# Gate products on GpSimd and a transposed first segment: one change to a fused attention and gated-MLP kernel

## The chip, the cores and the metric

The kernel runs on one core of a Trainium2 chip. The metric is the device time of one execution in microseconds (us); the time of a kernel is the median of several executions. One execution is also recorded by the hardware profiler, and all engine times below come from that record. Engine names in the profile: PE is TensorE (matmul), PEld its weight loads, DVE is VectorE, ACT is ScalarE, POOL is GpSimd, SP is SyncE; a q behind a name is that engine's instruction queue, where DMAs are issued.

## The reference, cut to what matters

One input x (2048 x 512) goes through two branches. Branch A is attention with 32 heads of width 16 in 4 segments of 512 rows, causal inside a segment, plus a running memory (M, z) of the earlier segments. Branch B is a gated MLP. A gate per row mixes them.

```python
g = sigmoid((x * gate_w).sum(-1, keepdims=True))        # one number per row
a = A(x)                                                # attention, below
b = (gelu(x @ w_gate) * (x @ w_up)) @ w_down
out = g * a + (1 - g) * b

def A(x):
    q, k, v = x @ wq, x @ wk, x @ wv                    # split in 32 heads, 4 segments
    gb = sigmoid(beta)                                  # one number per head
    for s in range(4):
        p = softmax(q_s k_s^T / 4 + causal mask)
        a_dot = p @ v_s
        num, den = phi(q_s) @ M, phi(q_s) @ z + 1e-06   # phi(t) = t + 1 if t > 0 else exp(t)
        out_s = gb * num / den + (1 - gb) * a_dot
        M += phi(k_s)^T @ v_s;  z += phi(k_s).sum()
    return concat(out_s) @ wo
```

## The kernel before

The kernel keeps x transposed in SBUF (xT), the weights, and the hidden layer of the MLP (G). Its phases: loads and the first keys; the queries and values of segment 0; the gate-weight matmuls with gelu for all segments (until about 79 us); then attention for the four segments, with the up and down matmuls of the MLP as filler between the attention steps; last the output of segment 3.

Every step is a task with an estimated cost, an engine, predecessors and a priority. A list scheduler runs through the tasks in modelled time and so decides, when the kernel is built, in which order each engine's instructions stand. Each engine then works strictly in that order.

```python
LAT = {"PE": 220, "ACT": 130, "DVE": 130, "POOL": 150, "SP": 0, "EXT": 0}
...
def ext(at):                      # a load, with the time at which the scheduler takes it as landed
    return add("EXT", 0, lambda e: None, lat=at)
```

The loads at the start, and the turning of x for segment 0 (the other segments are turned by transposing DMAs):

```python
for h, eng in enumerate((nc.sync, nc.scalar)):
    eng.dma_start(xn[:, 2 * h:2 * h + 2, :], x0r[:, 2 * h:2 * h + 2, :])
for h, eng in enumerate((nc.sync, nc.scalar)):
    eng.dma_start(wk[:, 2 * h:2 * h + 2, :], wkr[:, 2 * h:2 * h + 2, :])
load_w(nc.sync, wq, A_wq)
nc.sync.dma_start(wga[:, :, 0:4 * P], wgr[:, :, 0:4 * P])
load_w(nc.sync, wv, A_wv)
nc.sync.dma_start(wga[:, :, 4 * P:DFF], wgr[:, :, 4 * P:DFF])
for s in range(1, NSEG):
    load_x(s)                     # 4 transposing DMAs each
nc.sync.dma_start(gw[:, :], gate_w.rearrange("(fc p) -> p fc", p=P))
nc.sync.dma_start(beta8[:, :], A_beta.rearrange("(c h) -> h c", h=8))
...
def first_k():
    ...
    # 7 matmuls on zeros ("warm"), then for each of 4 column blocks fc:
    for kt in range(KT):
        nc.tensor.matmul(tl["x", fc][:, kt * P:(kt + 1) * P],
                         lhsT=xn[:, kt, fc * P:(fc + 1) * P], rhs=ident,
                         start=True, stop=True)
    # copied to xT by VectorE and ScalarE in turn; then the key matmuls
```

One head group of attention: ScalarE's exponential of the logits (L617), a causal mask on GpSimd (`affine_select`, L626), the product with the values on TensorE ("pv"; a column of ones in v gives the softmax sum), then on VectorE:

```python
nc.vector.transpose(TT[key][:, e, :, :]..., t[:, :])            # L664: from PSUM
nc.vector.reciprocal(RR[key], TT[key][:, :, :, DH:DH + 1])      # L674: 1 / softmax sum
nc.vector.tensor_mul(RR[key][:, :, :, 0], RR[key][:, :, :, 0],  # L677: the gate factor
                     G2[:, s, :][:, None, :].to_broadcast((P, 2, QB)))
nc.vector.tensor_mul(NN[key], TT[key][:, :, :, 0:DH],           # L682: normalise
                     RR[key].to_broadcast((P, 2, QB, DH)))
nc.vector.tensor_add(NN[key], NN[key], NMt[key])                # L687: add the memory part
nc.vector.transpose(xT[:, c, s * L:(s + 1) * L], NN[key]...)    # L690
```

G2 holds the gate's factor per row. Once per segment the memory's reciprocal gets the same factor (L815), used by the products L838:

```python
nc.vector.reciprocal(RMt[s], RMt[s])                            # L812
nc.vector.tensor_mul(RMt[s], RMt[s],                            # L815
                     G2[:, s, :][:, :, None].to_broadcast((P, QB, 8)))
```

Phi is made by ScalarE and VectorE, and a sum of 1024 numbers per partition on GpSimd (L720).

Of the kernel before, what the change touches and what calls it, by code (L numbers as in the profile page):

```python
# [10 lines left out]
BF = dt.bfloat16  # L11
F32 = dt.float32

P = 128
# [5 lines left out]
L = 512  # L20
# [135 lines left out]
def kernel(  # L156
# [15 lines left out]
    nc = tc.nc  # L172
# [13 lines left out]
    plg = ctx.enter_context(tc.tile_pool(name="plg", bufs=3, space=bass.MemoryType.PSUM))  # L186
# [7 lines left out]
    add = S.add  # L194
# [4 lines left out]
    def lgtile(name="lg"):  # L199
        return plg.tile([P, 2, L], F32, name=name, tag="lg")  # L200

    def gen(name):
        return pgen.tile([P, L], F32, name=name, tag="gen")
# [11 lines left out]
    wv = ctile("wv", [P, FC, D])  # L215
# [29 lines left out]
    def load_w(eng, t, src):  # L245
        eng.dma_start(t[:, :, :], src.rearrange("(fc p) n -> p fc n", p=P))
# [13 lines left out]
    for h, eng in enumerate((nc.sync, nc.scalar)):  # L260
        eng.dma_start(wk[:, 2 * h:2 * h + 2, :], wkr[:, 2 * h:2 * h + 2, :])
    load_w(nc.sync, wq, A_wq)
    nc.sync.dma_start(wga[:, :, 0:4 * P], wgr[:, :, 0:4 * P])
    load_w(nc.sync, wv, A_wv)
    nc.sync.dma_start(wga[:, :, 4 * P:DFF], wgr[:, :, 4 * P:DFF])
    for s in range(1, NSEG):
        load_x(s)
# [5 lines left out]
    def ext(at):  # L273
        return add("EXT", 0, lambda e: None, lat=at)
# [1 line left out]
    a_xn = ext(3600)  # L276
    a_x = [None, ext(18000), ext(22000), ext(26000)]
    a_wk, a_wq = ext(3800), ext(5500)
    a_wg0, a_wv, a_wga, a_gw, a_be, a_wup, a_wo = [ext(t) for t in (8500, 10000, 14000, 27000,
                                                                    27500, 32000, 39000)]  # L280

    nc.gpsimd.memset(ident, 1.0)
    nc.gpsimd.affine_select(out=ident, in_=ident, pattern=[[-1, P]],
# [92 lines left out]
    def first_k():  # L376

        tl = {}

        def f_warm(_):  # L380
            t = lgtile("warm")
            for i in range(NWARM):
                nc.tensor.matmul(t[:, 0, :], lhsT=warm[:, 0:P], rhs=warm,
                                 start=True, stop=True)
        w = add("PE", 427 * NWARM, f_warm, prio=0, alloc=["lg"])
        add("EXT", 0, lambda _: None, deps=[w], frees=[("lg", w)])

        def f_open(_):
            a = lgtile("xt")
            for i in range(2):  # L390
                tl["x", i] = a[:, i, :]
                tl["x", 2 + i] = gen("xt")[:, :]
            for i in range(2):
                tl["k", i] = lgtile("k0")
                QK[("k", 0, i)] = rtile("kT", [P, 2, L])
        op = add("PE", 1, f_open, prio=0, deps=[w], alloc=["lg", "gen", "gen", "lg", "lg",
                                                          "kT", "kT"])
        xe = []
        prev = op
        for fc in range(FC):  # L400
            def f_t(_, fc=fc):
                for kt in range(KT):
                    nc.tensor.matmul(tl["x", fc][:, kt * P:(kt + 1) * P],
                                     lhsT=xn[:, kt, fc * P:(fc + 1) * P], rhs=ident,
                                     start=True, stop=True)
            prev = add("PE", 430, f_t, prio=1, deps=[prev, a_xn])
            xe.append(add("ACT" if fc % 2 else "DVE", 600,
                          lambda e, fc=fc: copy(e, xT[:, fc, 0:L], tl["x", fc]), prio=0,
                          deps=[prev], frees=[(("lg", 0), op) if fc < 2
                                              else (("gen", fc - 2), op)]))  # L410
        a_x[0] = xe[-1]
        TAB["wdn"] = add("SP", 600, lambda _: load_w(nc.sync, wdn, B_w_down), deps=[prev],
                         lat=40000)
        last = None
        for fc in range(FC):
            def fn(_, fc=fc):
                for c in range(NCH):
                    nc.tensor.matmul(tl["k", c // 2][:, c % 2, :],
                                     lhsT=wk[:, fc, c * P:(c + 1) * P], rhs=xT[:, fc, 0:L],
                                     start=(fc == 0), stop=(fc == FC - 1))  # L420
            last = add("PE", 4 * MM, fn, prio=2, deps=[last, xe[fc], a_wk])
            read_x[0].append(last)
        for c in range(NCH):
            first_ev[("k", 0, c // 2)] = op
            EVQK[("k", 0, c)] = add(["DVE", "ACT"], [EV["DVE"], EV["ACT"]],
                                    lambda e, c=c: copy(e, QK[("k", 0, c // 2)][:, c % 2, :],
                                                        tl["k", c // 2][:, c % 2, :]),
                                    prio=0, deps=[last], frees=[(("lg", 1 + c // 2), op)])
            odd_copy(0, c, EVQK[("k", 0, c)])
# [17 lines left out]
    TAB = {}  # L447
# [186 lines left out]
    def pv_group(s, c, e):  # L634
        g0 = s * NSLOT + 5 * c
        w0 = 0 if e == 0 else 3
        t0 = 5 * c

        def mms(t):

            for w, kt, qb, nq, at in ((w0, 0, 0, 4, 0), (w0 + 1, 1, 1, 2, 0),
                                      (w0 + 1, 1, 3, 1, 3), (2, 2, 2, 2, 2 * e),
                                      (w0 + 1, 3, 3, 1, 2)):
                for j in range(4):
                    h = 8 * c + 2 * j + e
                    nc.tensor.matmul(t[32 * j:32 * j + 32, qb * P:(qb + nq) * P],  # L646
                                     lhsT=vz[s % 2][:, kt, h * VW:h * VW + 32],
                                     rhs=pT[(s, t0 + w, j // 2)][:, j % 2, at * P:(at + nq) * P],
                                     start=(kt == 0), stop=(kt == KT - 1),
                                     tile_position=(0, 32 * j), skip_group_check=True)  # L650
        slots = [w0, w0 + 1, 2]
        deps = [AT[(g0 + w, h)] for w in slots for h in range(2)]
        deps += [EVV[(s, kt)] for kt in range(KT)] + [opened]
        if e == 1:
            deps.append(PVT[s][-1])
        def mk():
            TT[(s, c)] = rtile("T", [P, 2, QB, 32], F32)
        g, box = group("pv", 600, mms, 0.5, deps, mode="col", also=("T", mk) if e == 0 else None,
                       frees=[("pT", XT_[(g0 + w, h)]) for w in slots for h in range(2)])
        PVT[s].append(g)  # L660
        key = (s, c)

        def f_T(_, t):
            nc.vector.transpose(TT[key][:, e, :, :].rearrange("p a b -> p (a b)"), t[:, :])  # L664
        ev = evac("DVE", g, box, f_T)
        if e == 0:
            NMT[("T", key)] = g
            NMT[("Te", key)] = ev
            return
        T0 = NMT[("T", key)]  # L670

        def f_r(_):
            RR[key] = rtile("r", [P, 2, QB, 1], F32)
            nc.vector.reciprocal(RR[key][:, :, :, :], TT[key][:, :, :, DH:DH + 1])  # L674

        def f_rg(_):
            nc.vector.tensor_mul(RR[key][:, :, :, 0], RR[key][:, :, :, 0],  # L677
                                 G2[:, s, :][:, None, :].to_broadcast((P, 2, QB)))

        def f_n(_):  # L680
            NN[key] = rtile("N", [P, QB, 2, DH])
            nc.vector.tensor_mul(NN[key][:, :, :, :].rearrange("p a e d -> p e a d"),  # L682
                                 TT[key][:, :, :, 0:DH],
                                 RR[key][:, :, :, :].to_broadcast((P, 2, QB, DH)))

        def f_m(_):
            nc.vector.tensor_add(NN[key][:, :, :, :], NN[key][:, :, :, :], NMt[key][:, :, :, :])  # L687

        def f_o(_):
            nc.vector.transpose(xT[:, c, s * L:(s + 1) * L],  # L690
                                NN[key][:, :, :, :].rearrange("p a e d -> p (a e d)"))
        r = add("DVE", 280, f_r, prio=3, deps=[ev, NMT[("Te", key)]], alloc=["r"])
        rg = add("DVE", 120, f_rg, prio=3, deps=[r, TAB["g2"]])
        n = add("DVE", 650, f_n, prio=3, deps=[rg], alloc=["N"], frees=[("r", r), ("T", T0)])
        last = n
        if s > 0:
            last = add("DVE", 500, f_m, prio=3, deps=[n, NMT[("Nm", key)]],
                       frees=[("Nm", NMT[("Nm", key)])])
        OTT[key] = add("DVE", 640, f_o, prio=3, deps=[last] + read_x[s], frees=[("N", n)])
# [90 lines left out]
    def mem_den(s, prio):  # L790
# [21 lines left out]
            nc.vector.reciprocal(RMt[s][:, :, :], RMt[s][:, :, :])  # L812

        def f_g(_):
            nc.vector.tensor_mul(RMt[s][:, :, :], RMt[s][:, :, :],  # L815
                                 G2[:, s, :][:, :, None].to_broadcast((P, QB, 8)))
        ev = evac("DVE", g, box, f_T)
        a = add("DVE", 200, f_a, prio=2, deps=[ev], alloc=["rm"], frees=[("Tm", g)])
        r = add("DVE", 880, f_r, prio=2, deps=[a])
        TAB[("rm", s)] = add("DVE", 250, f_g, prio=2, deps=[r])  # L820
        TAB[("rma", s)] = a

    def mem_num(s, c, prio):
# [176 lines left out]
```

The softmax here doesn't subtract the row's maximum and nothing guards it: scores larger than these inputs give would overflow.

## Time and profile before

| | us |
|---|---|
| median of 3 runs | 290.62 (290.55 to 290.92) |
| span of the profiled execution | 289.2 |
| PE busy | 272.9 |
| DVE busy | 178.9 |
| ACT busy | 208.5 |
| POOL busy | 130.4 |

Busy is the time in which an engine had at least one instruction under way. Groups of instructions are named by line, engine and operation, then out<-in by the program's own tile names, with the count and the mean duration. A wait is named by the engine that waited and what ended it. Idle time of an engine costs something only where the engine is on the path that sets the end. The lines that carry the reading stand in the prediction.

### The profile page before, as it was taken

How to read it: one execution, taken by the hardware profiler on the slowest of the kernel's cores; microseconds unless marked ns; L12 is line 12 of the kernel's file. 1: busy time of each engine (PE TensorE's matmuls, PEld its weight loads, DVE VectorE, ACT ScalarE, POOL GpSimd, SP SyncE). 2: the span in 40 equal slices, each digit the busy share in tenths (PEclk: the TensorE clock that was granted, in tenths of full speed). 3: DMA queues.
4: the chain of work that ended last, by engine and by line, in shares of the span. 5: the costliest groups of instructions: out<-in, count | busy, mean ns of one | idle time of the engine just before them, and what ended most of it. 6: DMA issues, size and time to landing. Idle time of an engine off the chain costs nothing.

```text
span 289.2 us, 5673 instructions
## 1 busy us (share of the span) xinstructions
PE 272.9 (94%) x2279; PEld 118.4 (41%) x2320; DVE 178.9 (62%) x320; ACT 208.5 (72%) x227; POOL 130.4 (45%) x220
## 2 busy tenths in 40 slices
PE   8999999999998997999989999998899999999994
PEld 4444444444433443343334444333344344344441
DVE  2331112232197899888997786789986973869400
ACT  3634554424497998699998998999899999896021
POOL 8000000015037786755497657554855855556000
PEclk9999999999999999999999999999999999999999
DMA  7974960000001110100001330000000000000011
GB/s 239 329 124 80 368 205 2 0 0 2 0 2 36 35 25 18 39 0 2 0 2 30 27 57 20 13 8 2 0 20 20 0 20 18 22 22 18 20 36 37
DMA packets 22019, 13.74 MB, mean 48 GB/s; under 512 B 14056, under 2 KB 20968, under 8 KB 21992
## 3 DMA queue, kind: packets, MB, share of 16 engines
q1 hardware_dynamic: 21448, 12.85, 16.9%
q10 hardware_dynamic: 544, 0.52, 0.5%
q8 instruction: 18, 0.29, 0.4%
q14 instruction: 9, 0.07, 0.1%
HBM read 8.13 MB, written 2.10 MB: 35 GB/s over the span
## 4 chain that ended last, share of the span: by engine, by line
PE 68%; DVE 19%; SPq 7%; DMA 2%; issue 2%; ACT 0%; ACTq 0%
PE dn L850 17%; PE up L336 14%; PE gt L336 12%; SPq L241 7%; PE lg L594 7%; PE pv L646 6%; PE dn L855 5%; PE k L336 2%; DVE T L664 2%; PE q L336 2%; DVE G L510 2%; DVE Nm L838 2%; DVE N L682 1%; DVE Tm L834 1%; DMA wdn<-in_A_x_dram 1%
## 5 line engine op out<-in xcount | busy, mean ns | idle before, releaser
L617 ACT ACTIVATE pT<-lg 128x1024 bf16<-128x1024 f32 x160 | 154.2, 1026 | 15.2 <-PE lg L594 14.2
L626 POOL TENSOR_SCALAR_AFFINE_SELECT pT<-pT 128x512 bf16<-128x512 bf16 (+1 forms) x160 | 93.5, 595 | 71.9 <-ACT pT L617 70.9
L510 DVE TENSOR_TENSOR G<-up,G 128x512 bf16<-128x512 f32 x56 | 38.0, 683 | 41.2 <-PE up L336 41.2
L336 PE MATMUL up<-xT,wup 128*128 128x512 bf16 x213 | 55.2, 380 | 3.1 <-DVE G L510 1.9
L500 ACT ACTIVATE G<-gt 128x1024 bf16<-128x1024 f32 x28 | 28.7, 1024 | 35.9 <-PE gt L336 35.9
L850 PE MATMUL dn<-wdn,G 128*128 128x512 bf16 x213 | 52.2, 380 | 1.9 <-DVE vz_84 L183 0.8
L336 PE MATMUL gt<-xT,wga 128*128 128x512 bf16 x217 | 50.9, 379 | 0.4
L336 PEld LDWEIGHTS <-wga 128*128 128x128 bf16 x224 | 21.8, 98 | 26.3
L336 PEld LDWEIGHTS <-wup 128*128 128x128 bf16 x224 | 19.9, 97 | 27.9 <-issue 8.2
L850 PEld LDWEIGHTS <-G 128*128 128x128 bf16 x224 | 20.2, 98 | 27.0 <-issue 5.9
L471 POOL COPY G_90<-tt 32x16 f32<-32x16 f32 x16 | 3.2, 197 | 56.9 <-DVE tt L463 56.3
L664 DVE STREAM_TRANSPOSE T<-pv 128x512 f32<-128x512 f32 x32 | 22.8, 712 | 9.0 <-PE pv L646 8.9
L594 PE MATMUL lg<-qT,kT 16*128 16x256 bf16 (+2 forms) x320 | 18.7, 273 | 0.1
L594 PE MATMUL lg<-qT,kO 32*128 32x128 bf16 (+2 forms) x320 | 18.0, 272 | 0.1
L434 PE MATMUL v<-wv,xT 128*128 128x512 bf16 x61 | 15.5, 379 | 2.7 <-DVE vz_85 L183 1.6
L855 PE MATMUL dn<-wo,xT 128*128 128x512 bf16 x63 | 16.2, 379 | 0.2 <-issue 0.2
L894 ACT ACTIVATE osb<-dn,omz 128x512 bf16<-128x512 f32 x6 | 4.1, 686 | 16.6 <-PE dn L855 16.6
L336 PE MATMUL q<-xT,wq 128*128 128x512 bf16 x59 | 15.4, 380 | 0.2
L594 PEld LDWEIGHTS <-kT 16*128 16x128 bf16 x320 | 7.3, 92 | 20.0 <-issue 19.3
L682 DVE TENSOR_TENSOR N<-T,r 128x512 bf16<-128x512 f32 x16 | 14.4, 899 | 0.3
L896 DVE TENSOR_SCALAR osb<-dn,omz 128x512 bf16<-128x512 f32 x10 | 7.5, 746 | 8.8 <-PE dn L855 6.7
L594 PEld LDWEIGHTS <-kO 32*128 32x128 bf16 x320 | 7.0, 92 | 14.0 <-issue 13.7
(117 smaller groups left out, 272.3 us busy)
## 6 DMA issues: line engine op xcount, KB each, us to landing
out_dram<-osb SPq DMA_DIRECT2D x16, 128.0 KB, 1.7
wup<-in_B_w_up_dram SPq DMA_DIRECT2D x1, 1792.0 KB, 8.0
wdn<-in_B_w_down_dram SPq DMA_DIRECT2D x1, 1792.0 KB, 13.6
wga<-in_B_w_gate_dram SPq DMA_DIRECT2D x1, 1280.0 KB, 11.0
wq<-in_A_wq_dram SPq DMA_DIRECT2D x1, 512.0 KB, 6.4
wga<-in_B_w_gate_dram SPq DMA_DIRECT2D x1, 512.0 KB
wv<-in_A_wv_dram SPq DMA_DIRECT2D x1, 512.0 KB, 8.3
wo<-in_A_wo_dram SPq DMA_DIRECT2D x1, 512.0 KB, 9.1
```

Source lines behind the costliest of these rows:

```text
L241: nc.sync.dma_start_transpose(xT[:, fc, s * L:(s + 1) * L], x2[s * L:(s + 1) * L, fc * P:(fc + 1) * P])
L336: nc.tensor.matmul(t, lhsT=W[:, fc, c0:c0 + P], rhs=xT[:, fc, s * L:(s + 1) * L], start=(fc == 0), stop=(fc == FC - 1))
L500: ge = evac("ACT", g, box, lambda e, t: nc.scalar.activation(dst, t[:, :, :], AF.Gelu_apprx_tanh), cost=960, ring="lg")
L510: UPT[(s, hs)] = evac("DVE", g, box, lambda e, t: nc.vector.tensor_mul(G[:, s, hs, :], t[:, :], G[:, s, hs, :]))
L594: nc.tensor.matmul(A[j // 2][:, j % 2, at * P:(at + nq) * P], lhsT=l, rhs=r, start=True, stop=True, tile_position=(32 * j, 0))
L617: nc.scalar.activation(pT[(s, t, h)][:, :, :], A[h][:, :, :], AF.Exp, scale=0.25)
L626: nc.gpsimd.affine_select(out=v, in_=v, pattern=pat, compare_op=ALU.is_ge, fill=0.0, base=0, channel_multiplier=-1)
L646: nc.tensor.matmul(t[32 * j:32 * j + 32, qb * P:(qb + nq) * P], lhsT=vz[s % 2][:, kt, h * VW:h * VW + 32], rhs=pT[(s, t0 + w, j // 2)][:, ...
L664: nc.vector.transpose(TT[key][:, e, :, :].rearrange("p a b -> p (a b)"), t[:, :])
L682: nc.vector.tensor_mul(NN[key][:, :, :, :].rearrange("p a e d -> p e a d"), TT[key][:, :, :, 0:DH], RR[key][:, :, :, :].to_broadcast((P, 2 ...
L850: nc.tensor.matmul(t[:, :], lhsT=G[:, s, hs, qt * P:(qt + 1) * P], rhs=wdn[:, hs, :], start=(hs == 0), stop=stop and (hs == HS - 1))
L855: nc.tensor.matmul(t, lhsT=xT[:, c, s * L + qt * P:s * L + (qt + 1) * P], rhs=wo[:, c, :], start=first and c == 0, stop=(c == NCH - 1))
```

## The change

Four things differ.

1. The product with the gate factor moves from VectorE to GpSimd, for the softmax reciprocal (16 instructions) and for the memory's reciprocal (3 instructions). Its aim is to relieve VectorE. Priority and costs given to the scheduler change with it.
2. x of segment 0 is turned by TensorE's transpose operation with bf16 results in PSUM, where plain matmuls with an identity gave fp32 results.
3. The first piece of the gate weights and wv are loaded from ScalarE's queue instead of SyncE's.
4. The landing times that the scheduler assumes for these two loads change (wv 10000 to 9000, the gate piece 8500 to 10500 ns).

```diff
     load_w(nc.sync, wq, A_wq)
-    nc.sync.dma_start(wga[:, :, 0:4 * P], wgr[:, :, 0:4 * P])
-    load_w(nc.sync, wv, A_wv)
+    nc.scalar.dma_start(wga[:, :, 0:4 * P], wgr[:, :, 0:4 * P])
+    load_w(nc.scalar, wv, A_wv)
...
-    a_wg0, a_wv, a_wga, a_gw, a_be, a_wup, a_wo = [ext(t) for t in (8500, 10000, 14000, 27000,
-                                                                    27500, 32000, 39000)]
+    a_wv, a_gw = ext(9000), ext(27000)
+    a_wg0, a_wga, a_be, a_wup, a_wo = [ext(t) for t in
+                                       (10500, 14000, 27500, 32000, 39000)]
...
-            a = lgtile("xt")
+            a = plg.tile([P, 2, 2 * L], BF, name="xt", tag="lg")
             for i in range(2):
-                tl["x", i] = a[:, i, :]
-                tl["x", 2 + i] = gen("xt")[:, :]
+                tl["x", i] = a[:, i, 0:L]
+                tl["x", 2 + i] = pgen.tile([P, 2 * L], BF, name="xt", tag="gen")[:, 0:L]
...
-                    nc.tensor.matmul(tl["x", fc][:, kt * P:(kt + 1) * P],
-                                     lhsT=xn[:, kt, fc * P:(fc + 1) * P], rhs=ident,
-                                     start=True, stop=True)
+                    nc.tensor.transpose(tl["x", fc][:, kt * P:(kt + 1) * P],
+                                        xn[:, kt, fc * P:(fc + 1) * P], ident)
...
         def f_rg(_):
-            nc.vector.tensor_mul(RR[key][:, :, :, 0], RR[key][:, :, :, 0],
+            nc.gpsimd.tensor_mul(RR[key][:, :, :, 0], RR[key][:, :, :, 0],
                                  G2[:, s, :][:, None, :].to_broadcast((P, 2, QB)))
...
-        rg = add("DVE", 120, f_rg, prio=3, deps=[r, TAB["g2"]])
+        rg = add("POOL", 250, f_rg, prio=-1, deps=[r, TAB["g2"]])
...
         def f_g(_):
-            nc.vector.tensor_mul(RMt[s][:, :, :], RMt[s][:, :, :],
+            nc.gpsimd.tensor_mul(RMt[s][:, :, :], RMt[s][:, :, :],
                                  G2[:, s, :][:, :, None].to_broadcast((P, QB, 8)))
...
-        TAB[("rm", s)] = add("DVE", 250, f_g, prio=2, deps=[r])
+        TAB[("rm", s)] = add("POOL", 400, f_g, prio=-1, deps=[r])
```

## The prediction

> **What bounds the kernel now.** I read the busy shares first.
>
> ```profile
> PE 272.9 (94%) x2279; PEld 118.4 (41%) x2320; DVE 178.9 (62%) x320; ACT 208.5 (72%) x227; POOL 130.4 (45%) x220
> ```
>
> TensorE is busy for 272.9 of 289.2 us, so no other engine sets the whole span. What can be won is TensorE's idle time, 16.3 us, and it is not spread evenly. The first 1.3 us and the last 4.1 us (final copy and store) are fixed. For the rest I cut the attention part, from 79 us on, at the places where VectorE changes between running without a pause and having pauses. Columns: stretch, its length, then busy time and instruction count of PE, PEld, DVE, ACT, POOL.
>
> ```profile
> 109.00:120.30 11.30, 9.13 (x62) 3.87 (x62) 11.29 (x19) 8.71 (x10) 7.25 (x9) 1.00 0.17 35
> ...
> 134.00:155.00 21.00, 19.03 (x182) 7.73 (x186) 20.89 (x38) 19.31 (x22) 12.99 (x19) 1.00 0.00 1
> 155.00:190.00 35.00, 34.58 (x360) 15.00 (x362) 25.49 (x46) 32.55 (x36) 23.57 (x35) 1.00 0.19 32
> 190.00:209.00 19.00, 16.93 (x174) 6.94 (x177) 18.66 (x34) 17.47 (x22) 11.96 (x16) 1.00 0.00 1
> ```
>
> In three stretches VectorE never stops (11.29 of 11.3, 20.89 of 21, 18.66 of 19), and TensorE idles 2.17, 1.97 and 2.07 us there, 6.2 us together. In the stretch between, VectorE has 9.5 us to spare and TensorE idles only 0.42 us in 35. So the bound is TensorE, with three places where VectorE holds it up. The view of TensorE's waits agrees: nearly every entry names VectorE.
>
> ```profile
> PE up L336 <- DVE G L510: 1.9, 5, 1.0
> PE v L434 <- DVE vz_85 L183: 1.6, 2, 1.1
> ...
> PE dn L850 <- DVE vz_84 L183: 0.8, 1, 0.8
> PE v L434 <- DVE T L664: 0.7, 1, 0.7
> ...
> PE bps L520 <- DMA beta_78<-in_A_beta_dram: 0.6, 1, 0.6
> ```
>
> The last of these is at 29.5 us: the small beta load comes behind twelve transposing loads of x on the same queue.
>
> **The operation that moves.** The gate product on the softmax reciprocal (L677) handles 32 numbers per partition. The views of its line and of the normalising product behind it give duration min/median/max:
>
> ```profile
> L677 DVE TENSOR_TENSOR r<-r,G_90 x16: 178/344/854, 99.9 to 271.2; 128x32 f32<-128x32 f32 x16
> ```
> ```profile
> L682 DVE TENSOR_TENSOR N<-T,r x16: 679/940/1152, 100.3 to 271.4; 128x512 bf16<-128x512 f32 x16
> ```
>
> One and the same instruction takes 178 or 854 ns. The timeline says why: at 111.10 us it starts just after a causal mask has started on GpSimd, and ends just after it.
>
> ```profile
> 111.10 0.65 DVE L677 TENSOR_TENSOR r<-r,G_90 128x32 f32<-128x32 f32 x1
> ```
> ```profile
> 111.07 0.64 POOL L626 TENSOR_SCALAR_AFFINE_SELECT pT<-pT 128x512 bf16<-128x512 bf16 x1 [0.28 <-ACT pT L617]
> ```
>
> At 99.88 us, with GpSimd idle, it took 0.18 us. The Trainium skill, "SBUF — State Buffer", section "SBUF: two separate sides", states this: VectorE with two SBUF inputs and GpSimd share an exclusive port pair, and the later one waits for the whole instruction of the other. The trace agrees, 178 ns free against some 600 ns beside a mask. L682 has two SBUF inputs as well, 679 free against up to 1152.
>
> **The change part by part.**
>
> *Gate products to GpSimd.* VectorE loses 16 x 405 ns (mean of L677) = 6.5 us and 3 x 262 ns (L815) = 0.8 us, 7.3 us in all. Most of that lies where VectorE has pauses, and is worth nothing. In the three full stretches lie five of the sixteen, which took 0.65, 0.50, 0.60, 0.61 and 0.62 us by the timeline, and two of L815 at 0.25: 3.5 us. That is the ceiling of this part, as TensorE's 6.2 us there is larger.
>
> GpSimd gains 19 instructions. Its product of 1024 numbers (L720) takes 2120 ns, about 2.07 ns a number; with some 0.15 us fixed (its 32x4 copies take 182 ns) I estimate 0.2 us for 32 numbers and 0.4 us for 128, so 16 x 0.2 + 3 x 0.4 = 4.4 us on an engine at 45%. It does not become the bound. What counts is the round trip: reciprocal on VectorE, product on GpSimd, normalising product on VectorE. GpSimd may first have to finish a mask (449 or 693 ns by form) or a 2.1 us sum. I estimate 0.3 to 1 us, against 0.18 to 0.85 before. In the built order of the changed program 14 of the 16 heads have other VectorE work, mostly an up product of about 0.68 us, between reciprocal and L682, which hides it or most of it; in two there is none. Also, the mask that follows the product on GpSimd starts just when L682 is released, so port collisions can move from L677 to L682. I let these two give back over half of the 3.5 us and keep 1.5 us.
>
> The new durations also make the list scheduler issue a different order on TensorE from about 100 us on (by the times of before). On TensorE the work is the same, and so is about the number of changes between groups, 261 runs against 259; 85 down and output matmuls instead of 70 follow the last value product, so the last head's chain is covered no worse. I count the new order as 0, with an uncertainty of 2 us.
>
> *The transposes of segment 0.* Before, 7 warming matmuls and 16 plain identity matmuls come ahead of the first key matmul:
>
> ```profile
> 1.26 3.17 PE L383 MATMUL warm<-wdn 128*128 128x512 bf16 x7 [1.26 <-DVE wdn L256]
> ...
> 4.22 1.91 PE L403 MATMUL xt<-wdn 128*128 128x128 bf16 x16
> ...
> 5.32 1.29 DVE L183 CAST xT<-xt 128x512 bf16<-128x512 f32 x2 [2.90 <-PE xt L403]
> ```
>
> The seven are 0.42 us apart ((4.22 - 1.26) / 7). The same form is 0.216 us apart from about 6.8 us on: the clock has doubled. The skill, "TensorE: Matmul & The Clock Gate", "Part 4: PE-mode transpose", says that transposes don't count as busy for this clock, and its Part 1 that the clock is decided in windows of about 3.4 us. The trace of before shows the doubling some 5.3 us after the first matmul, but has no transposes to test the rest. If it holds, the clock doubles one window later, and 3.4 us of work at half speed costs 1.7 us, at the very place where TensorE is the bound. I give this 0.4: +0.7 us. The transposes themselves cost the same, 16 weight loads and 16 passes of 128 columns.
>
> Their result is now bf16 in PSUM. "VectorE: DVE Perf Modes", "Why PSUM operands drop a tier", allows two elements a cycle for 16-bit PSUM sources, one for fp32. By that the 686 ns copy becomes about 0.42 us (256 instead of 512 cycles at 0.96 GHz; an estimate from that page, no run here shows it). The first key matmul waits for the first copy, so it starts 0.27 us sooner, of which half counts at the half clock: -0.15 us.
>
> *Loads.* The first gate-weight piece and wv go out on the queue of ScalarE. That takes two issues of about 0.5 us from its free start, before its first work at 6.04 us. "DMA: Bandwidth & Descriptors", "Queues, rings and completion order", says that a DMA engine goes round-robin between queues. So wq (landing 1.82 + 6.4 = 8.2 us before) shares bandwidth with the gate piece, and may come up to 1.5 us later, near its first use at 9.83 us: +0.1 us. The SyncE queue has 1 MB less ahead of the x transposes and beta; the 0.56 us wait at 29.5 us should mostly go, also because a late TensorE would not meet it: -0.4 us.
>
> Sum: 290.6 - 1.5 + 0.7 - 0.15 + 0.1 - 0.4 = 289.35, rounded to 289.4 us.
>
> **The rivals.**
>
> *VectorE's relief comes through whole.* For it: TensorE's waits name VectorE, and 6.2 us of idle lie in full stretches. Against: the port collisions stay with L682. Time: -3.5 instead of -1.5, about 287.3 us; with a lucky order 286.
>
> *GpSimd becomes a wait of its own.* The product stands in GpSimd's queue at a place fixed in advance. If VectorE is late with the reciprocal, the masks behind it wait, then the value products on TensorE. VectorE does run later than the scheduler's costs say (an evacuation 712 ns against 610). Against: GpSimd idles 71 us waiting for ScalarE's exponentials, so it catches up. If it happened at every second head with 0.4 us: +3 us in place of -1.5, about 294 us less what buffers hide, so 292.
>
> *The slow clock alone counts.* The whole 1.7 us instead of 0.7, no gain in attention: 292 us.
>
> *Nothing reaches TensorE.* The waits only change names: 290 to 291 us.
>
> **Range and chances.** The terms are all below 2 us, and 2% is 5.8 us. The ceiling of the gain, 3.5 + 0.4 + 0.15 = 4.1 us, stays below it unless the new order helps too; a loss of 5.8 us needs the slow clock, GpSimd stalls and a bad order together. Hence 286.2 to 292.4 us for 8 in 10, faster by over 2% 0.06, slower by over 2% 0.03, the rest within.
>
> **What would show it.** Right: VectorE's busy time lower by 5 to 7 us and GpSimd's higher by 4 to 5; L677 on GpSimd near 0.2 us; TensorE's idle time in the full stretches down by 1 to 2 us; the bps wait smaller; the first copy near 0.42 us. Wrong: L682 clearly longer than its 899 ns mean, GpSimd waiting for the reciprocal, TensorE waiting in front of pv; key and query matmuls 0.43 us apart after 7 us (clock); a wait for wq. The prediction as a whole fails if the new order opens or closes TensorE waits that have nothing to do with the gate product.

## The result, and the profile after

| | before | changed |
|---|---|---|
| median, us | 290.60 | 294.27 |
| ratio to before (95% interval) | | 1.0126 (1.0113 to 1.0139) |
| span of the profiled execution, us | 289.2 | 292.3 |

The change costs 3.7 us. The time lies outside the predicted range (286.2 to 292.4), and on the other side of before than forecast.

The head of the page, which answers to the first line of the prediction:

```profile
PE 273.8 (94%) x2279; PEld 118.7 (41%) x2320; DVE 172.2 (59%) x299; ACT 209.4 (72%) x229; POOL 134.3 (46%) x239
```

VectorE has lost 6.7 us (178.9 to 172.2) and GpSimd gained 3.9 (130.4 to 134.3), as meant. The span grew all the same. The moved products and the normalising product behind them (duration min/median/max in ns, and who waited):

```profile
L677 POOL TENSOR_TENSOR r<-r,G_90 x16: 246/252/418, 99.2 to 271.1; 128x32 f32<-128x32 f32 x16
...
  DVE r L674: 6.7, 4
...
  DVE N L682: 1.4, 3
```
```profile
L815 POOL TENSOR_TENSOR rm<-rm,G_90 x3: 404/405/406, 139.0 to 252.0; 128x128 f32<-128x128 f32 x3
```
```profile
L682 DVE TENSOR_TENSOR N<-T,r x16: 691/922/2283, 99.5 to 271.4; 128x512 bf16<-128x512 f32 x16
```

VectorE waits for these products only 1.4 us in all, in three places. GpSimd waits 6.7 us for the reciprocals ahead of them, but 4.4 us of it before the very last product, with no mask behind it. So the round trip is not where 3 us went. The waits of TensorE, first five entries:

```profile
PE v L434 <- DVE vz_85 L183: 1.4, 2, 1.1
PE up L337 <- DVE G L510: 1.3, 2, 1.1
PE warm L384 <- DVE wdn L256: 1.3, 1, 1.3
PE k L337 <- DVE T L664: 0.9, 1, 0.9
PE dn L850 <- issue: 0.6, 4, 0.2
```

Most are the same kind of wait as before, on VectorE's reading results out of PSUM, some smaller and some new. No single one is worth 3 us.

What does show the loss is the end. TensorE's timeline around the last value product (start us, length us, what; first before, then changed):

```profile
269.25 0.73 PE L646 MATMUL pv<-pT,vz_85 128*32 128x512 bf16 x20
269.91 1.04 PE L850 MATMUL dn<-wdn,G 128*128 128x512 bf16 x4
270.78 1.03 PE L855 MATMUL dn<-wo,xT 128*128 128x512 bf16 x4
271.65 3.19 PE L850 MATMUL dn<-wdn,G 128*128 128x512 bf16 x13
```
```profile
269.13 0.73 PE L646 MATMUL pv<-pT,vz_85 128*32 128x512 bf16 x20
269.80 4.27 PE L850 MATMUL dn<-wdn,G 128*128 128x512 bf16 x18
273.91 1.03 PE L855 MATMUL dn<-wo,xT 128*128 128x512 bf16 x4
274.77 0.59 PE L850 MATMUL dn<-wdn,G 128*128 128x512 bf16 x2
```

Attention ends at the same time in both, the last value product beginning at 269.25 and 269.13 us. What follows is, in the built order, 70 matmuls before and 85 in the changed kernel: 15 x 0.216 = 3.2 us, within 0.1 us of the difference of the spans. TensorE has the same 2320 matmuls in total; in the changed kernel it got 15 fewer filling matmuls done between the attention steps, and did them at the end. This says where the time shows, and not yet why fewer were done.

At the start (the two copies of the last line take 420 ns each in the mean):

```profile
4.22 1.47 PE L404 MATMUL xt<-wdn 128*128 128x128 bf16 x16
...
5.28 0.76 DVE L183 COPY xT<-xt 128x512 bf16<-128x512 bf16 x2 [2.86 <-PE xt L404]
```

### The profile page after: what moved, and what is told of

The parts are those of the page before. It is cut to its first block, busy times and chain, and to the rows that moved or that the text cites. A ratio compares the mean times of both kernels' runs of the same rounds, so it can differ in the third digit from the quotient of the medians.

```text
span 292.3 us, 5665 instructions
## 1 busy us (share of the span) xinstructions
PE 273.8 (94%) x2279; PEld 118.7 (41%) x2320; DVE 172.2 (59%) x299; ACT 209.4 (72%) x229; POOL 134.3 (46%) x239
## 4 chain that ended last, share of the span: by engine, by line
PE 68%; DVE 21%; DMA 3%; ACT 3%; issue 2%; POOL 1%; ACTq 0%
PE dn L850 17%; PE gt L337 17%; PE up L337 13%; PE lg L594 6%; PE pv L646 5%; PE dn L855 5%; DMA wga<-in_B_w_gate_dram 3%; DVE N L682 3%; DVE T L664 3%; DVE G L510 2%; PE q L337 2%; PE v L434 2%; DVE qT L183 2%; ACT pT L617 2%; DVE Mbd L777 1%
## 5 line engine op out<-in xcount | busy, mean ns | idle before, releaser
L894 ACT ACTIVATE osb<-dn,omz 128x512 bf16<-128x512 f32 x8 | 5.5, 686 | 19.1 <-PE dn L855 19.1
L682 DVE TENSOR_TENSOR N<-T,r 128x512 bf16<-128x512 f32 x16 | 15.3, 956 | 1.5 <-POOL r L677 1.4
L337 PE MATMUL k<-xT,wk 128*128 128x512 bf16 x44 | 11.7, 380 | 1.1 <-DVE T L664 0.9
```

The source lines that it names most:

```text
L337: nc.tensor.matmul(t, lhsT=W[:, fc, c0:c0 + P], rhs=xT[:, fc, s * L:(s + 1) * L], start=(fc == 0), stop=(fc == FC - 1))
```

## The experiments

Two theories stood after the result. *Engine*: GpSimd's round trip, its queue and the port collisions cost the time. *Order*: the scheduler, given other costs and another engine for 19 tasks, issues another order on all engines, and that order is worse. Ratios below are to the kernel before run beside each, with 95% intervals.

### Engine against order (s1 to s4)

The scheduler's choice of an engine and the instruction that a task issues can be set apart, since both are lines of the kernel. s3 plans the products for GpSimd and executes them on VectorE; s4 does the reverse.

s1, the start alone: the changed kernel, with the gate products planned and executed as before.

```diff
-            nc.gpsimd.tensor_mul(RR[key][:, :, :, 0], ...    # and RMt
+            nc.vector.tensor_mul(RR[key][:, :, :, 0], ...
-        rg = add("POOL", 250, f_rg, prio=-1, ...             # and rm
+        rg = add("DVE", 120, f_rg, prio=3, ...
```

> The transposes, the loads and the assumed landing times as in the changed kernel, the gate products on VectorE as before; the order of instructions on TensorE is that of before. In the trace of the changed kernel the gate matmuls after bps begin at 29.10 us instead of 29.63. Both theories (the engine of the gate product costs the time; the new order costs it) expect 290.1 us, 0.5 less than before. If it is above 291, the start is part of the loss after all.

Measured: 1.0016 (1.0000 to 1.0032).

s2, the gate products alone: the kernel before with the reverse of that diff.

> The gate products on GpSimd alone, start as before; the order on TensorE is that of the changed kernel. Both theories expect the whole loss and no gain at the start: 294.3 + 0.5 = 294.8 us.

Measured: 1.0123 (1.0069 to 1.0177).

s3, the order of the changed kernel, products on VectorE:

```diff
 # the changed kernel; the two add("POOL", ...) stay
-            nc.gpsimd.tensor_mul(RR[key][:, :, :, 0], ...    # and RMt
+            nc.vector.tensor_mul(RR[key][:, :, :, 0], ...
```

> The changed kernel with its order of instructions kept (the scheduler still plans the gate products as GpSimd tasks), but the products executed by VectorE. Theory engine (GpSimd's queue, waiting for the reciprocals with the masks behind it, and port collisions moved to the normalising product): the loss goes, 290 to 290.5 us. Theory order (the list scheduler's new order puts steps of TensorE at worse places): the loss stays, 293.5 to 295 us.

Measured: 1.0170 (1.0116 to 1.0224).

s4, the order of before, products on GpSimd:

```diff
 # the kernel before; the two add("DVE", ...) stay
-            nc.vector.tensor_mul(RR[key][:, :, :, 0], ...    # and RMt
+            nc.gpsimd.tensor_mul(RR[key][:, :, :, 0], ...
```

> The kernel before with its order of instructions kept (the scheduler still plans the gate products as VectorE tasks), but the products executed by GpSimd. Theory engine: the loss appears, 293 to 295 us. Theory order: no loss, 289 to 291 us, VectorE's relief of some 7 us perhaps giving 1 us.

Measured: 1.0012 (0.9990 to 1.0035).

| | order of before | order of the changed kernel |
|---|---|---|
| products on VectorE | 1 (by definition) | 1.0170 (s3, with the new start) |
| products on GpSimd | 1.0012 (s4) | 1.0123 (s2), 1.0126 with the new start |

The loss goes with the order, whichever engine executes the products: the intervals of s2 and s3 lie wholly above that of s4. The theory of the engine falls. In s4 VectorE did wait for GpSimd, nine times:

```profile
L682 DVE TENSOR_TENSOR N<-T,r x16: 682/708/1121, 100.1 to 271.7; 128x512 bf16<-128x512 f32 x16
...
  POOL r L677: 6.2, 9
```

Those 6.2 us cost next to nothing in the total. The start brings no gain: s1 is 0 to 0.9 us above before.

### Is the order of before a lucky one? (l1 to l4)

The scheduler computes in modelled time when its plan ends: 285.7 us for before, 288.7 for the changed kernel. That is a number of the plan, from its own rough costs, and no measurement, but it moves the right way. Changing one planned cost by 10 ns moves it as much.

l1:

```diff
 # the kernel before
-        rg = add("DVE", 120, f_rg, prio=3, deps=[r, TAB["g2"]])
+        rg = add("DVE", 110, f_rg, prio=3, deps=[r, TAB["g2"]])
```

> The kernel before with one number changed: the planned cost of the gate product on VectorE 110 instead of 120 ns. Not one instruction differs, only the order. The end of the scheduler's own plan goes from 285.7 to 288.4 us, as it goes to 288.7 in the changed kernel. Theory plan (the order of before was a lucky one, and any change of a cost draws another; the plan's end tells its worth): 292.5 to 294 us. Theory gate (the loss of the new order has to do with where the gate products stand): within 0.5 us of before, as nothing moved engine.

Measured: 1.0122 (1.0097 to 1.0148). A number that no instruction uses costs as much as the whole change. This order is no unrelated one: like that of the changed kernel it leaves 85 matmuls after the last value product (in the built order), and its plan ends almost as late, at 288.4 us.

l2, products on GpSimd, with planned costs picked for the earliest end of the plan (two of the lines):

```diff
-        return add("POOL", 2250, f_a, prio=5, ...
+        return add("POOL", 2480, f_a, prio=5, ...
-        rg = add("POOL", 250, f_rg, prio=-1, ...
+        rg = add("POOL", 280, f_rg, prio=-1, ...
```

> The gate products on GpSimd, start as before, and the planned costs of 10 tasks changed by up to 12% so that the plan ends at 284.6 us, the lowest found. Theory plan: 290.6 - 1.1 from the shorter plan - up to 1.5 from VectorE's relief, 288 to 289.5 us, the fastest so far. Theory gate (GpSimd products make a bad order whatever the plan says): 293 to 295 us.

Measured: 0.9990 (0.9979 to 1.0002). Better than the changed kernel by 1.4%, but the gain over before that the shorter plan promised is missing.

l3, products on GpSimd, with the copies out of PSUM and the normalising product planned nearer to their measured times, and seven other planned costs changed by up to 11% (main lines):

```diff
-    EV = {"DVE": 610, "ACT": 560}
+    EV = {"DVE": 630, "ACT": 560}
-        n = add("DVE", 650, f_n, prio=3, ...                 # normalising product
+        n = add("DVE", 750, f_n, prio=3, ...
-        rg = add("DVE", 120, f_rg, prio=3, ...
+        rg = add("POOL", 240, f_rg, prio=-1, ...
```

> The gate products on GpSimd, with a plan that counts the normalising product near its measured time (750 instead of 650 ns) and evacuations at 630, and ends at 285.2 us. Theory plan: 288 to 290 us, and no more than 0.5 us above the plan with the lower costs; if a plan nearer to the measured costs is worth more than a short one, it is the fastest of the four. Theory gate: 293 to 295 us.

Measured: 0.9941 (0.9919 to 0.9963), the first that beats before. l4, products on VectorE, eight planned costs changed by up to 10%:

> The gate products on VectorE as before, with planned costs of 8 tasks changed by up to 10% so that the plan ends at 285.0 us, 0.8 below before. Theory plan: 289.5 to 290.5 us. If it is above 292, the plan's end does not tell the measured time and the order of before was good for another reason.

Measured: 0.9982 (0.9960 to 1.0005).

So before is not an exceptionally good order: l2 and l4 come out like it, and l3 better. The slow ones are the two whose plans end at 288.4 and 288.7 us.

### What does a worse order cost, and where? (m1 to m4, n3)

m1 leaves out part of the down projection: its time is that of a kernel with less work.

```diff
         for hs in range(lo, hi):
+            if s < NSEG - 1 and hs % 2:
+                continue
             nc.tensor.matmul(t[:, :], lhsT=G[:, s, hs, ...
```

> The changed kernel in its own order, but every second down matmul of segments 0 to 2 left out (84 of 224, 18.1 us of TensorE at 0.216 us each; some 7 of them after the last value product). Theory chain (from 79 us to the last value product the logits, exponentials and masks set the pace, and TensorE's other work is filling): the last value product begins no earlier than 262 us, against 269.6. Theory TensorE (its work sets the pace there): it begins some 16 us earlier, near 253 us.

TensorE's timeline:

```profile
260.51 0.73 PE L646 MATMUL pv<-pT,vz 128*32 128x512 bf16 x20
```

Neither theory holds. Ahead of the last value product 77 matmuls, 16.6 us, were left out. The way from the first logits to it took 260.5 - 79.3 = 181.2 us instead of 269.1 - 77.8 = 191.4: 10.2 us less (one profile each). TensorE's own work set the pace for more than half of what was taken away; the rest brought no gain.

m2, the order of l3 with the products on VectorE (the engine lines changed as in s3):

> The fastest kernel so far (gate products on GpSimd, plan with the normalising product at 750 ns) with its order kept, but the gate products executed by VectorE. If the move to GpSimd is worth something by itself: slower by 0.7 to 2 us, as in the order of the changed kernel (s3 against s2). If it is worth nothing: the same within 0.5 us, as in the order of before (s4 against before).

Measured: 0.9981 (0.9962 to 1.0000), against 0.9941 with GpSimd: 0.4%, 1.2 us, for the move itself; the intervals only just touch.

m3, l3 with the transposes and loads of the changed kernel:

> The fastest kernel so far with the transposes and the loads of the changed kernel; the order on TensorE is the same. If the 0.5 us that the trace shows at 29 us lasts: 288.8 us. If the start is worth nothing or a little loss, as the times of s1 say: 289.3 to 289.8 us.

Measured: 0.9918 (0.9893 to 0.9942), which overlaps l3. The start stays unproven.

m4 and n3 are two more plans of the kind of l3, drawn with planned costs a few per cent different, to see if the number of matmuls left at the end tells the time.

> Gate products on GpSimd, planned costs as in the fastest kernel but for some of up to 10%; the plan ends at 285.3 us (the fastest: 285.2), with 70 matmuls after the last value product instead of 53. Theory tail (the last value product comes near 270 us in every order, and what is left then decides): 270 + 70 x 0.216 + 4.2 = 289.3 us of span, some 2 us above the fastest, as before. Theory plan (the plan's end decides): within 0.7 us of the fastest, 289 to 290 us, a span of some 287.4.

> Gate products on GpSimd, another plan drawn from planned costs a few per cent different, ending at 285.6 us with 53 matmuls after the last value product. Theory tail: last value product at 271.5 us as in the other plan with 53 left, span 271.5 + 53 x 0.216 + 4.2 = 287.2 us, 0.994 of before. If the fastest owed its time to something else in its one order: 289 us of span or more.

Measured: m4 1.0033 (1.0006 to 1.0060), span 289.7 against the 289.3 expected. n3 1.0009 (0.9995 to 1.0023), span 289.9 against 287.2: with 53 left like l3, its last value product came only at 273.7 us, where l3 had it at 271.0.

```profile
273.68 0.73 PE L646 MATMUL pv<-pT,vz 128*32 128x512 bf16 x20
```

So the count left at the end is half of the account. The other half is when attention ends, which is no constant: in the runs with all their matmuls the last value product began between 266.7 us (o2, below) and 273.7 us (n3). Nor does a small difference in the end of the plan tell (285.2 in l3 and 285.3 in m4, 0.9941 and 1.0033 measured). A large one did: with whole sums, the six orders whose plans end between 284.6 and 285.7 us measured 0.992 to 1.003 in all their runs, the two that end 2.7 and 3.0 us after that of before 1.012 to 1.017.

### Port collisions with GpSimd's long sums (n1, n2, o1 to o3)

Within the changed kernel two of VectorE's products run into GpSimd's sums of 1024 numbers (L720). VectorE's and GpSimd's timeline, then TensorE's:

```profile
104.56 1.92 DVE L777 TENSOR_TENSOR Mbd<-Macc,bdeb 128x512 bf16<-128x512 f32 x1
...
112.64 2.28 DVE L682 TENSOR_TENSOR N<-T,r 128x512 bf16<-128x512 f32 x1
```
```profile
103.81 2.12 POOL L720 TENSOR_TENSOR pkT<-E,Q_1035 128x1024 bf16<-128x1024 bf16 x1
...
112.26 2.12 POOL L720 TENSOR_TENSOR pkT<-E,Q_1183 128x1024 bf16<-128x1024 bf16 x1
```
```profile
115.58 1.02 PE L337 MATMUL up<-xT,wup 128*128 128x512 bf16 x4 [1.14 <-DVE G L510]
```

The product N, 0.69 us alone, is under way for 2.28 us, from 0.4 us after the start of the sum; the up product behind it on VectorE is late, and TensorE idles 1.14 us for it. Each sum was cut in two, in five kernels:

```diff
-            nc.gpsimd.tensor_add(d[:, :, :], box["E"][:, :, :], box["Q"][:, :, :])
+            for i in range(2):
+                nc.gpsimd.tensor_add(d[:, i, :], box["E"][:, i, :], box["Q"][:, i, :])
```

> The changed kernel with GpSimd's sums of 1024 numbers issued as two of 512; TensorE's order is unchanged. If the collisions of VectorE's products with the 2.1 us sums make a part of the loss: the longest such product falls from 2.28 to about 1.3 us, and the kernel gains 1 to 2 us, 292.5 to 293.5 us. If they are hidden behind the rest: within 0.4 us of the changed kernel's 1.0126 of before.

> The fastest kernel so far (gate products on GpSimd, plan with 53 matmuls left, transposes and loads of the changed kernel, 0.9918 of before) with the same halved sums. If the collisions count: 288 to 288.5 us on the scale of before at 290.6, some 0.5 us less. If not: the same within 0.3 us.

> The kernel before with GpSimd's sums of 1024 numbers issued as two of 512. If the collisions with long sums are what the order of the changed kernel has and that of before has not: within 0.3% of before. If both carry them (five VectorE products beside sums in before, 5.2 us of waiting together): 0.5 to 1% faster, and the collisions don't explain the difference between the orders.

> The kernel with the planned cost of 110 ns (1.0122 of before, gate products on VectorE), with halved sums. If collisions explain every slow order: about 1.003, as in n1. If that order is slow for another reason (its products lose only 3.8 us beside sums, less than the 5.2 of before): above 1.007.

> The order of the changed kernel with the gate products executed by VectorE (1.017 of before), with halved sums. If the collisions of Mbd and N with the sums make that order slow: about 1.007, the same 1% less as n1. If not: above 1.012.

| order | sums whole | sums halved (95%) |
|---|---|---|
| changed kernel (n1) | 1.0126 | 1.0029 (1.0015 to 1.0044) |
| changed kernel, products on VectorE (o3) | 1.0170 | 1.0071 (1.0055 to 1.0086) |
| planned cost 110 (o2) | 1.0122 | 1.0014 (0.9992 to 1.0037) |
| before (o1) | 1 | 0.9928 (0.9908 to 0.9948) |
| m3 (n2) | 0.9918 | 0.9890 (0.9868 to 0.9913) |

In n1 the longest normalising product fell from 2.28 to 1.31 us, though two half sums take longer than one whole (2 x 1.15 against 2.12 us):

```profile
L682 DVE TENSOR_TENSOR N<-T,r x16: 679/926/1312, 99.7 to 270.1; 128x512 bf16<-128x512 f32 x16
```
```profile
L721 POOL TENSOR_TENSOR pq<-E,Q x12: 1150/1152/1160, 90.2 to 231.8; 128x512 bf16<-128x512 bf16 x12
```

Long sums are a real cost, but one that both orders carry. Cutting them gains 1.0% in the changed kernel and 0.7% in before. That it is the collisions which cost, and not something else about a long instruction on GpSimd, rests on the shorter products; no run separates the two. Between the two kernels it explains some 0.25 of the 1.26%: with halved sums everywhere the changed kernel is still 1.0029 / 0.9928 = 1.010 of before. That o2 gains as much as n1 was not expected, since its products lose less beside sums than those of before.

n2 beats both kernels, 1.1% below before and 2.3% below the changed one: gate products on GpSimd, planned costs of l3, new start, halved sums.

### What stays open

Which places make up the remaining 1.0% between the orders. The traces of s1 and s2 hold all 2320 matmuls, where those of before and of the changed kernel lack 41. Their busy times, first s1 (span 289.4 us), then s2 (292.5 us):

```profile
PE 276.1 (95%) x2320; PEld 118.3 (41%) x2320; DVE 178.8 (62%) x320; ACT 208.7 (72%) x227; POOL 129.2 (45%) x220
```
```profile
PE 277.6 (95%) x2320; PEld 119.3 (41%) x2320; DVE 172.6 (59%) x299; ACT 209.4 (72%) x229; POOL 134.2 (46%) x239
```

Of the 3.1 us, only about half is more waiting of TensorE; the other half, 1.5 us, is that the same matmuls are busy longer in this order (the logits alone 34.7 instead of 33.6 us). s4 and s3, with the engines of the products exchanged, give the same picture by order: 275.8 and 277.8 us busy. The ends of matmuls are modelled in these records, so the halves are rough, and why the matmuls take longer is not shown.

Where the waiting lies is seen by stretch (stretch, length, busy time and count of PE, PEld, DVE, ACT, POOL); first s1, then s2:

```profile
140.00:180.00 40.00, 38.55 (x405) 16.43 (x403) 33.23 (x60) 37.15 (x41) 28.08 (x39) 1.00 0.16 25
180.00:200.00 20.00, 18.89 (x194) 7.51 (x187) 16.95 (x31) 18.71 (x22) 10.09 (x18) 1.00 0.02 8
200.00:240.00 40.00, 39.21 (x418) 16.58 (x417) 31.11 (x52) 36.74 (x41) 26.77 (x39) 1.00 0.03 11
```
```profile
140.00:180.00 40.00, 37.17 (x397) 15.69 (x393) 30.97 (x54) 37.17 (x42) 29.35 (x41) 1.00 0.13 24
180.00:200.00 20.00, 19.67 (x206) 8.02 (x199) 15.23 (x27) 19.14 (x22) 12.86 (x23) 1.00 0.03 10
200.00:240.00 40.00, 38.26 (x412) 16.25 (x410) 29.54 (x52) 36.84 (x41) 25.82 (x42) 1.00 0.03 11
```

TensorE is busy 1.4 us less in 140 to 180 us, 0.95 less in 200 to 240, and 0.8 more between; VectorE is less busy in all three, so it is not that VectorE has become the bound there. I read it as many places where TensorE's next step stands in its queue a little before VectorE has emptied the buffer for it. That is argued from the list of waits; no run isolates one of them.

## Why the prediction was wrong

**The step that failed** is the sentence "I count the new order as 0, with an uncertainty of 2 us", and the reading just before it that 85 instead of 70 matmuls after the last value product mean "the last head's chain is covered no worse". The measured worth of the order is 1.0123 / 1.0012 = 1.011 with the products on GpSimd (s2 against s4), 3.2 us, and 1.0170 / 1.0016 = 1.015 with them on VectorE (s3 against s1), 4.5 us, each with an uncertainty of some 1.7 us from the intervals. The 15 further matmuls at the end, 3.2 us, were the loss itself standing in the issue order: less filling was done before attention ended. m4 and n3 add that such a count needs the end of attention beside it; here that end was the same within 0.1 us. "On TensorE the work is the same" holds for the matmuls and not for their time: s2 is busy 1.5 us longer than s1. The scheduler's own plan, 3.0 us longer for the changed kernel, had the sign and nearly the size of the loss.

The uncertainty was too small as well: l1 shows that an order made with no change of any instruction can cost 3.5 us. A new order is not always worse. Of the seven others measured here, two are 1.2 to 1.3% slower (the changed kernel, l1), four lie within 0.4% of before (l2, l4, m4, n3), and one is 0.6% faster (l3).

**The reading of TensorE's idle time.** The 16.3 us, and the 6.2 us in three full stretches, were read from a trace that lacks 41 matmuls. s1, with the order of before and a complete trace, has 289.4 - 276.1 = 13.3 us, and 5.5 us in these stretches. The ceilings were a little high; the sum of the prediction does not hang on it.

**Gate products: -1.5 us predicted.** The size holds, where the order was planned for it: -1.2 us in n1 against o3 (1.0029 and 1.0071, intervals apart) and -1.2 us in l3 against m2. In the order of before it is nothing (s4): there VectorE's busy time fell only from 178.8 (s1) to 175.6 us, and TensorE's idle time in the three full stretches only from 5.5 to 5.0 us. So that the gain comes by the path that was predicted, relief of VectorE in full stretches, is not shown. The estimates of 0.2 and 0.4 us an instruction met 0.252 and 0.405. L682 did not become clearly longer: 899 to 956 ns in the mean.

**The clock: +0.7 us predicted**, the whole 1.7 with a chance of 0.4. It did not come. In the changed kernel the sixteen transposes took 1.47 us instead of 1.91, because the clock doubled in their midst. In the eight profiles with transposes the doubling came at 4.8 to 7.1 us, in the twelve with plain matmuls at 3.9 to 7.0. It never came a window later. In the changed kernel the first eight transposes stand 107 ns apart and the last ones 56, so the full clock did engage during transposes; the Trainium skill, "TensorE: Matmul & The Clock Gate", "Part 4: PE-mode transpose", says that it does not, and the measurement decides. Whether transposes count as busy for the clock stays open, as the warming matmuls stand ahead of them in every run.

**The bf16 copy: -0.15 us predicted** from 0.42 us a copy. The trace has 0.420. No run shows what that is worth in the total.

**Loads: +0.1 and -0.4 us predicted.** In the profile of the changed kernel the beta wait is gone from the list of TensorE's waits. In its place stands one that I had not on the list, for the gate piece itself rather than for wq:

```profile
11.62 1.90 PE L337 MATMUL gt<-xT,wga 128*128 128x512 bf16 x7 [0.52 <-DMA wga<-in_B_w_gate_dram]
```

The shorter wait for beta is not to be counted on either. Other profiles with the same loads have the beta wait again (0.8 us in n1, 1.6 in n2, 0.6 in o3; 0.6 before), n1 and o3 the wait for the gate piece (0.7 and 0.8 us), and n2 a wait of 0.5 us for wq.

The start as a whole was forecast at 0.7 - 0.15 + 0.1 - 0.4 = +0.25 us; s1 has 0 to 0.9.

**The rivals.** "GpSimd becomes a wait of its own" gave a time near the measured one for a reason that s4 refutes. None of the rivals named the order; only the last sign of being wrong did, new waits that have nothing to do with the gate product.

## What to carry to other kernels

Where a scheduler turns estimated costs into an issue order, every edit of a cost or an engine is two changes: the operation, and a new order. Measure them apart by planning one way and executing the other, and take a change of one cost that nothing executes as the yardstick. Look at the end of the scheduler's own plan: here plans that ended 2.7 and 3.0 us later ran 3.5 and 3.7 us longer, while differences under 1.2 us told nothing. Count, in the built order, what filling work is left after the last step of the main chain, and read it together with when that chain ends.

Where VectorE's two-input products run beside long GpSimd instructions, cut the latter: a sum of 2.1 us in two halves gained 0.7 to 1.1% in four of five kernels here, and 0.3%, within the noise, in the fifth.

## What the runs showed of the hardware that was not expected

- A VectorE product of 0.69 us beside a GpSimd sum of 2.12 us was under way for 2.28 us, and the queue behind it with it.
- The gate product of 128x32 takes 0.25 us on GpSimd, and 0.18 on VectorE when nothing runs beside it: for so few numbers the difference is 0.07 us.
- From profile to profile of these kernels the doubling of TensorE's clock wanders over some 3 us (3.9 to 7.1); the first query matmul began between 9.2 and 10.0 us.
